# Linear attention and a squared-ReLU layer: the first product's last two blocks placed among the small steps of A11 B11

## The chip, the core and the metric

The kernel runs on one core of one Trainium2 chip. The metric is the device time of one execution in microseconds, as the median of three runs. The profile is of one further execution.

## What is computed

Linear attention over 8 batches, 8 heads, 576 positions and heads of 64, its normed result as the 4608 x 512 input of a layer with a squared ReLU:

```python
kv = np.einsum('bhsd,bhse->bhde', k, v)
out = np.einsum('bhsd,bhde->bhse', q, kv)
rms = np.sqrt(np.mean(out * out, axis=-1, keepdims=True) + 1e-06)
attn = (out / rms * g_norm).astype(np.float32)
x = np.ascontiguousarray(attn.transpose(0, 2, 1, 3)).reshape(B * S, H * D)
h = x @ w_in                  # 4608 x 512 by 512 x 2048
r = np.maximum(h, 0.0)
g = s * (r * r) + b
return (g @ w_out).astype(np.float32)   # 4608 x 2048 by 2048 x 512
```

Everything is fp32. In the profile a matrix product of `x` with `w_in` is the first product, and that of the squared ReLU with `w_out` the second; `s` and `b` are folded in where the second product is drained.

## The kernel before

**Units.** The 4608 rows are worked through in nine units of 512 rows, u = 0 to 8. Each unit has its first product (`mm1`) and then its second (`mm2`); between the pieces of the second product of unit u stands the attention for the rows of unit u + 1. Unit 8 has no next unit, and so no attention.

**Both products are cut into seven.** Instead of the eight products of a 2 x 2 block matrix product the kernel makes seven, from sums and differences of blocks. The seven are numbered 1 to 7 and run in the order 1, 2, 6, 7, 5, 3, 4. They share three PSUM accumulators: x takes 1, 6, 5 and 3 one upon the other, z takes 2, and y takes 7 and 4. Between two of them VectorE or ScalarE drains the state of x that belongs to an output block. The names of the steps say which accumulator they use: `x1`, `z2`, `x6`, `y7`, `x5`, `x3`, `y4`.

**The first product** of a unit goes over four column strips s = 0 to 3. In a strip each of the seven is a group of eight TensorE instructions with 256 columns. Its results are four blocks, `a11`, `a12`, `a21`, `a22`, and each becomes its own squared ReLU on VectorE: `a11` comes out of z2, `a22` out of x5 (an addition in L594 of PSUM accumulator y and a kept copy `r4`, and a square in L595, whose helper is L523), `a21` out of x3 and `a12` out of y4. The kept copies `r1`, `r2`, `r4` are made by ScalarE (L568). From the blocks the second product needs sums as well: `s1` = a21 + a22, and x3's last line turns a21 into a11 - a21. In strips 0 to 2, x3 and y4 of a strip are put between the steps of the next strip. Strip 3 has no next strip: there its x3 and y4 are put into the second product.

**The second product** of units 2 to 8 is cut into seven once more for four of its seven (1, 2, 7 and 4), in the function `second_level`. These small products have groups of eight instructions with 128 columns, and what they sum up is made on VectorE by `sums` into a ring of five tiles called `sub`. The text below calls the first of the four (block 1 of the upper level, from a11) A11 B11, its program name is `p1`, and the second (block 2, from a12) A12 B21, program name `p2`. Step m of `p1` is `p1[m]`. `sums` makes four operands, for the steps 5, 6, 7 and 3. A drain is one VectorE operation in L660; its results are `r` (kept for a later drain) or `o` (a part of the output).

**The order of the work** is written out by hand: the program's order is the order on each engine, and each engine works through its own queue. A wait comes in only where an operand or a buffer requires it. In units 2 to 8 the end of the first product of strip 3 and the start of the second product were:

```python
def sums_ahead():            # after y7 of strip 3, ahead of x5
    p1["sums"]()
    turn[0]()
    turn[1]()
```

Then came x5 of strip 3; then A11 B11's steps 1, 2, 6, 7 and 5; then x3 and y4 of strip 3, each with all of its VectorE work at once; then A11 B11's step 3, A12 B21's sums for 5 and 6, step 4, attention's product for the next unit (`product_q[0]`, with a square on ScalarE and a reduction on VectorE), A12 B21's step 1, the sum for 7, step 2, the sum for 3, step 6, and so on. `turn` is the turning of a part of q on VectorE (L391).

**Weights of the second product** come from device memory into a ring of seven tiles, in the order in which they are used. `pump(2)` puts two loads into SyncE's queue; each waits until TensorE is done with the tile that it overwrites. A group of attention matmuls in the timeline is L421.

Of the kernel before, what the change touches and what calls it, by code (L numbers as in the profile page):

```python
# [1 line left out]

# [8 lines left out]
AF = mybir.ActivationFunctionType  # L11
# [4 lines left out]
def kernel(  # L16
# [39 lines left out]
    nc = tc.nc  # L56
# [171 lines left out]
    def add(o, a, b):  # L228
        nc.vector.tensor_tensor(out=o, in0=a, in1=b, op=ALU.add)  # L229

    def sub(o, a, b):
        nc.vector.tensor_tensor(out=o, in0=a, in1=b, op=ALU.subtract)  # L232
# [274 lines left out]
    ga, g_pair = {}, {}  # L507
    bank = {}

    def bank_of(key, tag, bufs=2):  # L510
        bank[key] = ps_f.tile([P, 2, TB], FP32, name=f"{tag}_ps", tag=tag, bufs=bufs)
        return bank[key]
# [9 lines left out]
    def relu_sq(t):  # L522
        nc.vector.scalar_tensor_tensor(t, t, 0.0, t, ALU.max, ALU.mult)  # L523

    def g_tile(name, s):
        if s % 2 == 0:
            g_pair[name, s // 2] = gp.tile([P, 2, 2, TB], FP32, name=name, tag=name)
        ga[name, s] = g_pair[name, s // 2][:, s % 2]
        return ga[name, s]

    def g_s1(s):
        add(ga["s1", s], ga["a21", s], ga["a22", s])
# [29 lines left out]
    def mm1(u, s):  # L562

        st = {}

        def keep(name, src, tag):
            st[name] = rp.tile([P, 2, TB], FP32, name=name, tag=tag)
            nc.scalar.copy(st[name], src)  # L568

        def x1():  # L570
            st["x"] = bank_of("x", "x")
            mm1_product(1, u, s, st["x"], True)
            keep("r1", st["x"], "ra")

        def z2():
            ps = bank_of("z", "z", 1)
            mm1_product(2, u, s, ps, True)
            t = g_tile("a11", s)
            add(t, ps, st["r1"])
            relu_sq(t)  # L580

        def x6():
            mm1_product(6, u, s, st["x"], False)
            keep("r2", st["x"], "rb")

        def y7():
            st["y"] = bank_of("y", "y")
            mm1_product(7, u, s, st["y"], True)

        def x5():  # L590
            mm1_product(5, u, s, st["x"], False)
            keep("r4", st["x"], "ra")
            t = g_tile("a22", s)
            add(t, st["y"], st["r4"])  # L594
            relu_sq(t)  # L595

        def x3():
            mm1_product(3, u, s, st["x"], False)
            t = g_tile("a21", s)
            nc.scalar.activation(t, st["x"], AF.Relu)  # L600
            nc.vector.tensor_mul(t, t, t)  # L601
            g_tile("s1", s)
            g_s1(s)
            sub(ga["a21", s], ga["a11", s], ga["a21", s])

        def y4():
            mm1_product(4, u, s, st["y"], False)
            t = g_tile("a12", s)
            add(t, st["y"], st["r2"])
            relu_sq(t)  # L610

        return dict(x1=x1, z2=z2, x6=x6, y7=y7, x5=x5, x3=x3, y4=y4)

# [5 lines left out]
    def twice(u, i):  # L621
        return u > 1 and i in TWICE
# [5 lines left out]
    def pump(k):  # L628

        for u, i, n in queue_w2[:k]:  # L630
            t = late["ring"].tile([P, 4 * HN], FP32, name="w2_sb", tag="w2")
            if twice(u, i):
                t = t.rearrange("p (m f n) -> p m f n", m=2, n=P)
                k2 = min(2, 7 - 2 * n)
                nc.sync.dma_start(out=t[:, :k2], in_=w3_dram[i][:, 2 * n : 2 * n + k2])
            else:
                t = t.rearrange("p (f n) -> p f n", n=HN)
                nc.sync.dma_start(out=t, in_=w2_dram[i][:, 4 * n : 4 * n + 4])
            ring[u, i, n] = t
        del queue_w2[:k]  # L640
# [2 lines left out]
    out_18 = out.rearrange("(b t j) n -> b j t n", t=32, j=JC)  # L643
    G_OF = {1: "a11", 2: "a12", 3: "a12", 4: "a22", 5: "s1", 6: "a11", 7: "a21"}

    def mm2(u, att=None):

        st = {}

# [241 lines left out]
        def right(name, j, q=slice(0, HN)):  # L891
            return rows(name, j)[:, HN:][:, q]

        p1 = second_level(1, lambda j, q: b2[:, q], lambda j, q: right("o1", j, q), "x")
        p2 = second_level(2, lambda j, q: right("o1", j, q), lambda j, q: rows("o1", j)[:, q])
# [36 lines left out]
            turn[0]()  # L932
            turn[1]()

        def first():
            for m in (1, 2, 6, 7, 5):
                p1[m]()
            pump(2)

        def second():  # L940
            p1[3]()
            p2["sums"]((5, 6))
            p1[4]()
            pump(2)
            product_q[0]()
            p2[1]()
            p2["sums"]((7,))
            p2[2]()
            p2["sums"]((3,))
            p2[6]()  # L950
            s2((0, 1))
            p2[7]()
            p2[5]()
            s2((2, 3))
            pump(2)
            norm[0]()
            p7["sums"]()
            x6_of(0)
            p2[3]()
            p2[4]()  # L960
            for j in range(2):
                left = rows("o1", j)[:, :HN]
                add(left, left, b_12)
            pump(2)
            attend(1)
            turn_x[0]()
            turn[2]()
            x6_of(1)
            pump(2)
            p7[1]()  # L970
            s4((0,))
            p7[2]()
            p7[6]()
            s4((1,))
            p7[7]()
            s4((2,))
            p7[5]()
            s4((3,))
            pump(2)
            attend(2)  # L980
            turn_x[1]()
            turn[3]()
            x5_of(0)
            p7[3]()
            with_7(0)
            p7[4]()
            pump(2)
            attend(3)
            turn_x[2]()
            x5_of(1)  # L990
            with_7(1)
            turn_x[3]()
            pump(2)
            p4["sums"]()
            x3(0)
            for m in (1, 2, 6, 7, 5):
                p4[m]()
            pump(2)
            x_sums_next[0]()
            x3(1)  # L1000
            pump(2)
            y4_of(0, 3)
            y4_of(1, 4)
            pump(2)

        return [sums_ahead, first, second]


    NU = FC // 2
# [158 lines left out]
    for u in range(U):  # L1168
        if u > 0:
            loads(u)  # L1170
        steps = [mm1(u, s) for s in range(NS)] if u > 0 else []
        slots = []
        for s, a in enumerate(steps):
            slots.append(a["x1"])
            if s:
                slots.append(steps[s - 1]["x3"])
            slots.append(a["z2"])
            if s:
                slots.append(steps[s - 1]["y4"])
            slots += [a["x6"], a["y7"], a["x5"]]  # L1180
        if u == 0:
            first_unit()
        side = side_of(u)
        second = mm2(u, side if u > 1 else None)
        if u > 1:
            ahead, *second = second
        for n, slot in enumerate(slots):
            slot()
            if u > 1 and n == len(slots) - 2:
                ahead()  # L1190
            if u == 1 and n in (1, 3, 5):
                for sums in sums_w_in((n + 1) // 2):
                    sums()
            if u in kv_due and n == 12:
                kv_product(kv_due[u])
            elif u + 1 in kv_due and n == 14:
                for i in range(2):
                    load_kv(kv_due[u + 1], i, late["kv"], tag="kv")
        if u > 1:
            side = {}  # L1200
        for n, slot in enumerate(second):
            slot()
            if u == 0:
                if n == 1:
                    for i in range(2):
                        load_kv(1, i, convp, tag="raw", bufs=3)
                    store_w2(1)
                    loads(0)
                    store_w2(5)
                elif n == 2:  # L1210
                    t2 = convp.tile([P, 4 * R * D], FP32, name="w_t2", tag="raw", bufs=3)
                    W2_AT[6] = t2[:, : FC // 2 * HN].rearrange("p (f n) -> p f n", n=HN)
                    for i in range(14, 16):
                        more(i)
                    sub_w_out(6, 3, 5)
                    store_w2(3, 2, 6)
            if n == 0 and u > 0:
                for step in ("x3", "y4"):
                    steps[-1][step]()
            for step in side.get(n, []):  # L1220
                step()
        if u == 0:
            tc_late()
            for i in range(2):
                load_kv(kv_due[1], i, late["kv"], tag="kv")
            pump(7)
# [30 lines left out]
```

## Time and profile before

| what | value |
|---|---|
| median of three runs | 966.7 us (965.61 to 966.81) |
| profiled run, its span on the core | 966.18 us, 964.3 us |
| granted TensorE clock, mean | 0.999 |
| TensorE matmuls, weight loads | 943.5 us (98%), 840.8 us (87%) |
| VectorE | 612.1 us (63%), 1100 instructions |
| ScalarE | 194.3 us (20%) |
| DMA | 151.09 MB, mean 157 GB/s |

A weight load (PEld in the profile) stands ahead of each matmul (PE) and overlaps the one before. In a line of the timeline the first number is the start in us, the second the time until the end of the last of the merged instructions, and x8 says that eight of them are merged; the bracket at the end, where there is one, is the idle time of that engine just before, and who ended it. In a line of the waits the three numbers are the total in us, how often, and the longest. Nearly all matmuls and additions are issued in helper functions (L90, L229, L232, L523, L660), so an instruction is told by its tiles: `y_ps<-xs,wb` is step 7 or 4 of the first product, `x_ps<-xT,ws` step 3 of it, `x_ps<-w_sb,a` and `x_ps<-w_sb,sub` are steps of the second product.

### The profile page before, as it was taken

Reading aid. Unit: us, or ns where it says so; the run is one execution under the profiler, and the core shown is the slowest. Engines: PE = TensorE matmul, PEld = TensorE weight load, DVE = VectorE, ACT = ScalarE, POOL = GpSimd, SP = SyncE. Lnnn points to the kernel's source line nnn. Section 1 sums busy time; section 2 is a strip of 40 time slices with the busy share of each in tenths; the row PEclk is TensorE's granted clock in tenths of the full one; section 3 lists DMA queues with packets and bytes.
Section 4 is the critical chain, followed back from the end, with each engine's and each line's share of the span. In section 5 each row is a group of like instructions: output and inputs, shape, how many; then the busy total and the mean of one; then the engine's idle time right before and its main releaser. Section 6 shows DMA issues by size and latency. Waiting matters only on the chain. (4 is left out here: it accounts for less than half of the span.)

```text
span 964.3 us, 17222 instructions
## 1 busy us (share of the span) xinstructions
PE 943.5 (98%) x7102; PEld 840.8 (87%) x7102; DVE 612.1 (63%) x1100; ACT 194.3 (20%) x366; POOL 6.7 (1%) x18
## 2 busy tenths in 40 slices
PE   7999999999999999999999999999999999999997
PEld 7888888888888898889888988899888988898897
DVE  2789767575548854786368735874488557864573
ACT  2773132101221111111210212021211111111100
POOL 2000000000000000000000000000000000000000
PEclk9999999999999999999999999999999999999999
DMA  9688829577754566155355555456135531551163
GB/s 243 203 280 251 269 77 276 114 227 247 204 107 132 180 196 131 51 195 180 91 121 177 187 138 115 127 191 182 27 95 182 181 68 52 190 188 53 33 207 99
DMA packets 131709, 151.09 MB, mean 157 GB/s; under 512 B 76592, under 2 KB 89136, under 8 KB 131504
## 3 DMA queue, kind: packets, MB, share of 16 engines
q1 hardware_dynamic: 128528, 148.22, 53.7%
q10 hardware_dynamic: 2784, 1.77, 0.8%
q8 instruction: 56, 0.92, 0.4%
q14 instruction: 21, 0.17, 0.1%
q0 software_dynamic: 320, 0.00, 0.0%
HBM read 125.83 MB, written 24.12 MB: 155 GB/s over the span
## 5 line engine op out<-in xcount | busy, mean ns | idle before, releaser
L90 PE MATMUL x_ps<-w_sb,a 128*128 128x256 f32 (+1 forms) x600 | 130.9, 371 | 0.0
L568 ACT COPY r<-x_ps 128x512 f32<-128x512 f32 x96 | 56.2, 585 | 332.4 <-PE x_ps L90 325.7
L90 PEld LDWEIGHTS x_ps<-w_sb,a 128*128 128x128 f32 x600 | 108.6, 190 | 15.2 <-issue 1.6
L90 PE MATMUL x_ps<-xs,ws 128*128 128x256 f32 x512 | 121.0, 379 | 0.0
L90 PE MATMUL y_ps<-xs,wb 128*128 128x256 f32 x512 | 120.9, 379 | 0.0
L90 PEld LDWEIGHTS x_ps<-xs,ws 128*128 128x128 f32 x512 | 97.3, 190 | 13.2
L90 PEld LDWEIGHTS y_ps<-xs,wb 128*128 128x128 f32 x512 | 97.3, 190 | 13.2
L229 DVE TENSOR_TENSOR a<-y_ps,r 128x512 f32<-128x512 f32 x64 | 44.0, 688 | 97.2 <-ACT r L568 96.4
L90 PE MATMUL y_ps<-w_sb,sub 128*128 128x128 f32 x728 | 90.0, 276 | 3.1 <-DVE r L660 3.1
L90 PEld LDWEIGHTS y_ps<-w_sb,sub 128*128 128x128 f32 x728 | 86.8, 192 | 5.5 <-DVE r L660 4.4
L90 PE MATMUL x_ps<-xT,wa 128*128 128x256 f32 x384 | 89.6, 380 | 0.1
L90 PEld LDWEIGHTS x_ps<-xT,wa 128*128 128x128 f32 x384 | 72.3, 190 | 10.2 <-ACT xT L470 0.5
L90 PE MATMUL y_ps<-w_sb,a 128*128 128x128 f32 (+1 forms) x472 | 70.3, 294 | 0.0
L523 DVE SCALAR_TENSOR_TENSOR a<-a 128x512 f32<-128x512 f32 x96 | 66.4, 692 | 3.3
L601 DVE TENSOR_TENSOR a<-a 128x512 f32<-128x512 f32 x32 | 22.1, 692 | 72.3 <-ACT a L600 72.3
L90 PEld LDWEIGHTS y_ps<-w_sb,a 128*128 128x128 f32 x472 | 63.8, 191 | 4.2 <-DVE o L660 1.2
L90 PE MATMUL x_ps<-xT,ws 128*128 128x256 f32 x256 | 61.1, 382 | 0.0
L90 PE MATMUL z_ps<-xT,wa 128*128 128x256 f32 x256 | 60.5, 379 | 0.0
L90 PE MATMUL x_ps<-w_sb,s 128*128 128x256 f32 x256 | 59.1, 384 | 0.0
L90 PEld LDWEIGHTS x_ps<-w_sb,s 128*128 128x128 f32 x256 | 47.4, 190 | 8.4 <-issue 2.6
L90 PEld LDWEIGHTS z_ps<-xT,wa 128*128 128x128 f32 x256 | 48.6, 190 | 6.6
L90 PEld LDWEIGHTS x_ps<-xT,ws 128*128 128x128 f32 x256 | 47.6, 190 | 6.3
(126 smaller groups left out, 1060.3 us busy)
## 6 DMA issues: line engine op xcount, KB each, us to landing
w_sb<-w SPq DMA_DIRECT2D x140, 512.0 KB, 4.3
kv_sb<-in_k_dram SPq DMA_DIRECT2D x30, 288.0 KB, 5.0
kv_sb<-in_v_dram SPq DMA_DIRECT2D x30, 288.0 KB, 6.2
w_raw<-in_moe_w_in_dram SPq DMA_DIRECT2D x8, 1024.0 KB, 7.1
w_raw<-in_moe_w_out_dram SPq DMA_DIRECT2D x8, 1024.0 KB, 5.7
w_sb<-w SPq DMA_DIRECT2D x28, 256.0 KB, 2.8
out_dram<-o SPq DMA_DIRECT2D x104, 64.0 KB, 1.8
q_sb<-in_q_dram SPq DMA_DIRECT2D x144, 32.0 KB, 2.2
```

The costliest lines, as they stand in the source:

```text
L90: nc.tensor.matmul(o, lhsT=lhsT, rhs=rhs, start=start, stop=stop, skip_group_check=True)
L229: nc.vector.tensor_tensor(out=o, in0=a, in1=b, op=ALU.add)
L523: nc.vector.scalar_tensor_tensor(t, t, 0.0, t, ALU.max, ALU.mult)
L568: nc.scalar.copy(st[name], src)
L601: nc.vector.tensor_mul(t, t, t)
```

## The change

In units 2 to 8 the order from x5 of strip 3 on is written anew. y4 of strip 3 goes between the steps 2 and 6 of A11 B11, and x3 stays behind step 5, now behind the `pump`. The VectorE work of the two is taken apart: of y4 the addition and the square (`y4_square`) are two pieces, and of x3 the ReLU, the square (`x3_square`), the sum s1 (`x3_s1`) and the difference (`x3_s3`) are four. The four sums of A12 B21 are made in one go behind x3. Strips 0 to 2, and the units 0 and 1, run the same pieces one after the other as before.

```diff
         def x3():
             mm1_product(3, u, s, st["x"], False)
-            t = g_tile("a21", s)
-            nc.scalar.activation(t, st["x"], AF.Relu)
-            nc.vector.tensor_mul(t, t, t)
+            nc.scalar.activation(g_tile("a21", s), st["x"], AF.Relu)
+
+        def x3_square():
+            nc.vector.tensor_mul(ga["a21", s], ga["a21", s], ga["a21", s])
+
+        def x3_s1():
             g_tile("s1", s)
             g_s1(s)
+
+        def x3_s3():
             sub(ga["a21", s], ga["a11", s], ga["a21", s])

         def y4():
             mm1_product(4, u, s, st["y"], False)
-            t = g_tile("a12", s)
-            add(t, st["y"], st["r2"])
-            relu_sq(t)
+            add(g_tile("a12", s), st["y"], st["r2"])
+
+        def y4_square():
+            relu_sq(ga["a12", s])
...
-        def first():
-            for m in (1, 2, 6, 7, 5):
-                p1[m]()
+        def all_of_it():
+            p1[1]()
+            p1[2]()
+            step["y4"]()
+            p1[6]()
+            step["y4_square"]()
+            p1[7]()
+            p1[5]()
             pump(2)
-
-        def second():
+            step["x3"]()
+            p2["sums"]()
             p1[3]()
-            p2["sums"]((5, 6))
+            step["x3_square"]()
             p1[4]()
+            step["x3_s1"]()
             pump(2)
             product_q[0]()
             p2[1]()
-            p2["sums"]((7,))
+            step["x3_s3"]()
             p2[2]()
-            p2["sums"]((3,))
             p2[6]()
             s2((0, 1))
             p2[7]()
```

The rest of the difference passes strip 3's steps into `mm2`, and calls the two parts `sums_ahead` and `all_of_it` from the loop over units.

More of the change, by code (lines that the diff above doesn't have):

```diff
@@ L1 @@
 from contextlib import ExitStack
+from functools import partial
 import concourse.bass as bass
@@ L607, in y4 @@
             mm1_product(4, u, s, st["y"], False)
-            t = g_tile("a12", s)
-            add(t, st["y"], st["r2"])
-            relu_sq(t)
-        return dict(x1=x1, z2=z2, x6=x6, y7=y7, x5=x5, x3=x3, y4=y4)
+            add(g_tile("a12", s), st["y"], st["r2"])
+        def y4_square():
+            relu_sq(ga["a12", s])
+        return dict(
+            x1=x1, z2=z2, x6=x6, y7=y7, x5=x5, x3=x3, x3_square=x3_square, x3_s1=x3_s1,
+            x3_s3=x3_s3, y4=y4, y4_square=y4_square,
+        )
     ring = {}
@@ L644, with mm2 @@
     G_OF = {1: "a11", 2: "a12", 3: "a12", 4: "a22", 5: "s1", 6: "a11", 7: "a21"}
-    def mm2(u, att=None):
+    def mm2(u, step=None, att=None):
         st = {}
@@ L1004, in second @@
             pump(2)
-        return [sums_ahead, first, second]
+        return sums_ahead, all_of_it
     NU = FC // 2
@@ L1171, with x3, y4 @@
         steps = [mm1(u, s) for s in range(NS)] if u > 0 else []
+        def x3(a):
+            for name in ("x3", "x3_square", "x3_s1", "x3_s3"):
+                a[name]()
+        def y4(a):
+            for name in ("y4", "y4_square"):
+                a[name]()
         slots = []
@@ L1175 @@
             if s:
-                slots.append(steps[s - 1]["x3"])
+                slots.append(partial(x3, steps[s - 1]))
             slots.append(a["z2"])
             if s:
-                slots.append(steps[s - 1]["y4"])
+                slots.append(partial(y4, steps[s - 1]))
             slots += [a["x6"], a["y7"], a["x5"]]
@@ L1183 @@
         side = side_of(u)
-        second = mm2(u, side if u > 1 else None)
-        if u > 1:
-            ahead, *second = second
+        second = mm2(u, steps[-1], side) if u > 1 else mm2(u)
         for n, slot in enumerate(slots):
@@ L1189 @@
             if u > 1 and n == len(slots) - 2:
-                ahead()
+                second[0]()
             if u == 1 and n in (1, 3, 5):
@@ L1199 @@
         if u > 1:
-            side = {}
+            second[1]()
+            continue
         for n, slot in enumerate(second):
@@ L1217 @@
             if n == 0 and u > 0:
-                for step in ("x3", "y4"):
-                    steps[-1][step]()
+                x3(steps[-1])
+                y4(steps[-1])
             for step in side.get(n, []):
```

## The prediction

> **What bounds the kernel now.** I read the page's busy times first, then the list of waits of TensorE's weight loads, then the timeline at the seven places that the change touches.
>
> ```profile
> PE 943.5 (98%) x7102; PEld 840.8 (87%) x7102; DVE 612.1 (63%) x1100; ACT 194.3 (20%) x366; POOL 6.7 (1%) x18
> ```
>
> TensorE is the bound: 943.5 of 964.3 us. VectorE has 612.1, so it costs only where TensorE stands and waits for one of its results. The waits say where:
>
> ```profile
> PEld x_ps L90 <- DVE r L660: 6.0, 7, 0.9
> ...
> PEld y_ps L90 <- DVE r L660: 4.4, 7, 1.0
> ...
> PEld y_ps L90 <- DVE o L660: 1.2, 6, 0.2
> ```
>
> Seven units (u = 2 to 8) use the two-level second product, and each stops twice on a "r" that VectorE drains out of PSUM. The third row is no loss to win: 0.20 us follows every group of attention matmuls (L421), whatever comes after it. The first stop, in unit 2:
>
> ```profile
> 294.93 0.58 ACT L568 COPY r<-x_ps 128x512 f32<-128x512 f32 x1 [2.92 <-PE x_ps L90]
> 295.46 0.97 PEld L90 LDWEIGHTS z_ps<-w_sb,a 128*128 128x128 f32 x8
> 295.55 0.69 DVE L229 TENSOR_TENSOR a<-y_ps,r 128x512 f32<-128x512 f32 x1
> ...
> 296.27 0.69 DVE L523 SCALAR_TENSOR_TENSOR a<-a 128x512 f32<-128x512 f32 x1
> ...
> 296.88 0.35 DVE L660 SCALAR_TENSOR_TENSOR r<-x_ps,s_col,b_row 128x128 f32<-128x128 f32 x1
> 297.28 0.97 PEld L90 LDWEIGHTS x_ps<-w_sb,sub 128*128 128x128 f32 x8 [0.85 <-DVE r L660]
> ```
>
> The bank of small step 1 is ready early, but its drain stands in VectorE's queue behind the block a22 (L229, L523), which had to wait for the end of x5 and ScalarE's copy. Unheld groups of 128 columns start 0.89 us apart (298.17, 299.06), so small step 6 was due at 295.46 + 0.89 = 296.35 and started at 297.28: stop A, 0.93 us. The second stop:
>
> ```profile
> 306.55 0.60 ACT L430 ACTIVATE xn<-x_ps 128x512 f32<-128x512 f32 x1 [3.96 <-PE x_ps L421]
> ...
> 307.86 0.68 DVE L432 TENSOR_REDUCE ss<-xn 128x8 f32<-128x512 f32 x1
> 308.45 0.34 DVE L660 SCALAR_TENSOR_TENSOR r<-y_ps,s_col,o 128x128 f32<-128x128 f32 x1
> ...
> 308.85 2.75 PEld L90 LDWEIGHTS y_ps<-w_sb,sub 128*128 128x128 f32 x24 [0.58 <-DVE r L660]
> ```
>
> Due at 307.29 + 0.89 = 308.18, started at 308.85: stop B, 0.67. VectorE is in a jam here: eight large operations start between 302.62 and 307.86, and the drain of step 1 of A12 B21 stands behind them. Unit 8 has no attention for a next unit to fill TensorE, and its B is larger:
>
> ```profile
> 917.02 2.09 PEld L90 LDWEIGHTS y_ps<-w_sb,a 128*128 128x128 f32 x16
> 919.03 0.97 PEld L90 LDWEIGHTS z_ps<-w_sb,a 128*128 128x128 f32 x8
> 920.98 2.75 PEld L90 LDWEIGHTS y_ps<-w_sb,sub 128*128 128x128 f32 x24 [0.97 <-DVE r L660]
> ```
>
> B is 920.98 - 919.92 = 1.06, and 16 loads took 2.09 in place of 1.86: 0.23 that small step 1 of A12 B21 waited for its bank, which y4's addition (917.41 to 918.09) holds. A is the same 0.93 in all seven (0.85 idle in each), B is 0.67 in six. In all 7 x 0.93 + 6 x 0.67 + 1.06 + 0.23 = 11.8 us.
>
> [...] step 6 stood still with y4's operands long in place, and the drain of step 1 waited behind a22. [...] the trace has 692 for the additions of s1 and 684 where an operand comes from PSUM. [...] the count of instructions stays, so cutting the chain between them adds nothing.
>
> **The change, part by part.** No arithmetic is added or removed. On TensorE one group of eight moves: y4's product, from behind x3 to between small steps 2 and 6. On VectorE a12's addition goes behind step 2's drain and its square behind step 6's; all four sums of A12 B21 go ahead of the drain of step 3; a21's square, s1 and difference are spread behind steps 3, 4 and 1. ScalarE's and SyncE's queues keep their order, GpSimd has nothing in these units, and neither y4 nor x3 issues a DMA.
>
> TensorE, unit 2, by start of group. A group of 256 columns behind one of 128 is followed after 1.63 (299.95 to 301.58), the next of 128 after 0.99 (303.31 to 304.30). Step 1 at 294.46, 2 at 295.46, y4 at 296.35, 6 at 297.98, 7 at 298.97, 5 at 299.86, x3 at 300.75, 3 at 302.38, 4 at 303.37, attention at 304.47 (1.10 later, as before), then steps 1, 2, 6 of A12 B21 at 305.48, 306.37, 307.26. Before, the last one was at 308.85: 1.59 gained if nothing holds.
>
> What could hold it. (1) y4 writes the bank that a22's addition reads, a wait that it did not meet before. The addition ends at 296.24, TensorE follows VectorE by 0.05 (297.23 to 297.28): 296.29 against 296.35. Queued behind y4 are steps 6, 7, 5. The margin is 0.06, so zero to 0.1. (2) Step 6 needs step 1's drain, still done at 297.23, against 297.98: free by 0.70. This is what removes A. (3) a12's addition waits for the end of y4, about 0.41 after the next group starts (301.58 to 301.99 for x3), so at 298.39, and stands ahead of step 6's drain. That is due at 298.97 + 0.31 = 299.28; VectorE is free again at 299.00. (4) Step 5 needs it at 299.86, it ends 299.63. The square fits between it and step 5's drain (301.06). (5) From there VectorE starts each operation as the trace shows: 0.26 after a small one, 0.60 to 0.61 after a large independent one, 0.72 where the next needs the result. Drains 301.06 and 301.45, sums 301.71, 302.43, 303.04, 303.64, drain 304.25, square 304.51, drain 305.12, s1 305.38, VectorE free at 305.99. (6) Now attention's square: 1.15 after the group starts (305.40 to 306.55), so 305.62; it ends 306.22, the reduction starts 306.25 and the drain of step 1 at 306.84, done 307.19. Step 6 may start at 307.24, due 307.26. B is gone with 0.02 to spare, so zero to 0.1 left. From here on both kernels have the same order with TensorE leading.
>
> The sums find their buffers: five in the ring, and the last three take those of steps 5, 6, 7 of A11 B11, ended by 301.1. The weight loads: the second tile for block x6 behind A12 B21 takes the place that step 3 frees (303.7), and is used at 311.7: 8.0 us in unit 2, and by the same count 7.1 in unit 8 (916.4 to 923.5). The longest landing of this kind in the trace is 5.8. Hidden.
>
> Unit 8, the same walk without attention: steps 5, x3, 3, 4 at 912.58, 913.47, 915.10, 916.09; steps 1, 2, 6 at 916.98, 917.87, 918.76. Drain of 5 at 913.79, sums 914.44 to 916.96, drain, square 917.22, drain, s1 918.09, drain of step 1 at 918.70, done 919.05, so step 6 at 919.10: 0.34 is left of B; the bank wait of 0.23 goes. Gain 920.98 - 919.10 = 1.88.
>
> Sum: 6 x 1.59 + 1.88 = 11.4; for the two margins I take off 0.1 in all, 11.3. The span of 964.3 becomes 953.0. The profiled run took 966.2, and the three timed ones 965.6 to 966.8 with median 966.7; taken off that, 955.4. A difference of 0.2% (2 us) is about what a measurement of this kernel can tell.
>
> **Rivals.** First, B stays: if VectorE goes throughout at its slowest shown spacing (0.39 behind a small operation, 0.73 behind a large one), the walk from 301.06 ends with step 6 at 308.13, a gain of 0.72 in place of 1.59, and in unit 8 at 920.13, a gain of 0.85: 6 x 0.72 + 0.85 = 5.2, so 961.5. Half way is 958.5. For it: the margin is 0.02. Against: the short spacings are in the trace for the same pairs of sizes. Second, y4's new wait takes the place of A: if VectorE has been kept by the two q transposes ahead of a22 (294.12 for 1.30, so until 295.42, against ScalarE's end of 295.51), the wait could grow by tenths; at most A comes back whole, 6.5 less, 960. Against: same instructions ahead as before. Third, slower: TensorE without pauses loses granted clock. [...] here one core runs, at 0.999, and between 210 and 285 us TensorE was busy for 75.00 of 75 us at a granted clock of 1.00. The point is a clock of 0.988, where 1.2% is lost; at 0.98 it ends at 955.4 x 0.999/0.98 = 974. Fourth, no change: the stops move to another place behind; nothing there is short in either order.
>
> **How the numbers follow.** Forecast 0.77 (954.2 to 956.4), B or A partly back 0.15 (to 961.5), no change 0.03, slower 0.05. Faster is 0.92. The range, 953.9 to 959.8, starts at all 11.8 won with the spread of the runs and reaches over more than half of the second case.
>
> **What would show it.** In the trace after, the weight loads' wait for "r" should fall from 10.4 us to under 1, unit 8 holding most of it; y4's loads should stand between z_ps and x_ps steps; unit starts should be 1.6 us closer together. A wait of y_ps for L229 over 0.1 per unit would prove (1) wrong; a "y_ps <- DVE r" of 0.5 in each unit, (5) or (6); equal waits gone but the same span, the whole reading.

## The result and the profile after

The changed kernel took 954.62 us (954.17 to 956.60) against 966.15 for the kernel before (965.34 to 966.81), medians of four executions with the profiled one counted in: a ratio of 0.9885, 95% interval 0.9868 to 0.9902, or 11.5 us less. The forecast was 955.4.

The helpers stand one line lower than before, the drain eleven lines (L660 is L671 now). The page's first line of busy times, and the one line on a drained "r" that the list of the weight loads' waits still has (total in us, times, longest):

```profile
PE 939.9 (98%) x7102; PEld 839.9 (88%) x7102; DVE 611.3 (64%) x1100; ACT 194.5 (20%) x366; POOL 6.7 (1%) x18
```

```profile
PEld y_ps L91 <- DVE r L671: 0.2, 1, 0.2
```

The same 1100 instructions of VectorE with about the same busy time (611.3 us, 612.1 before); 10.4 us of waits have become 0.2. (The 1.2 us on a drained "o" is no longer put down to VectorE, but the pause of 0.20 behind the attention matmuls is still there, as forecast: in unit 2 the load at 307.33 has it.) The two places in unit 2, from the timeline (start, time to the end of the last, instruction, idle before and releaser):

```profile
297.30 0.97 PEld L91 LDWEIGHTS z_ps<-w_sb,a 128*128 128x128 f32 x8
297.39 0.69 DVE L230 TENSOR_TENSOR a<-y_ps,r 128x512 f32<-128x512 f32 x1
...
298.20 1.60 PEld L91 LDWEIGHTS y_ps<-xs,wb 128*128 128x128 f32 x8
...
298.73 0.34 DVE L671 SCALAR_TENSOR_TENSOR r<-x_ps,s_col,b_row 128x128 f32<-128x128 f32 x1
...
299.82 1.08 PEld L91 LDWEIGHTS x_ps<-w_sb,sub 128*128 128x128 f32 x8
...
308.10 0.69 DVE L433 TENSOR_REDUCE ss<-xn 128x8 f32<-128x512 f32 x1 [0.19 <-ACT xn L431]
...
308.70 0.34 DVE L671 SCALAR_TENSOR_TENSOR r<-y_ps,s_col,o 128x128 f32<-128x128 f32 x1
...
309.11 2.76 PEld L91 LDWEIGHTS y_ps<-w_sb,sub 128*128 128x128 f32 x24
```

Unit 2's step 1 starts at 296.31 here and at 294.46 before, so the forecast's walk, its list of start times, has to be moved by 1.85. y4 starts at 298.20 (walk: 298.20), with no wait on a22's addition. The drain of step 1 is as late as ever behind that addition, but while it runs TensorE is at y4; step 6 follows at 299.82 (walk: 299.83) and no weight load waited. At the second place attention's square on ScalarE holds the reduction for 0.19, the drain follows at 308.70 (308.69), and step 6 of A12 B21 starts at 309.11 (309.11), just when it is due. Unit 8 keeps the one wait, 11.91 us behind its step 1 where the walk had 11.92:

```profile
910.25 0.97 PEld L91 LDWEIGHTS z_ps<-w_sb,a 128*128 128x128 f32 x8
911.46 2.75 PEld L91 LDWEIGHTS y_ps<-w_sb,sub 128*128 128x128 f32 x24 [0.23 <-DVE r L671]
```

The kv groups of two units that follow each other were 102.94 us apart (269.86, 372.80) and are 101.36 apart (271.71, 373.07): 1.58 per unit. The profiled span, 954.8, is only 9.5 below that of before. The rest is the 1.85 by which unit 2 began later in this one execution, for reasons that lie ahead of any changed instruction. Two weight loads from the start of the kernel before, and the same two after the change:

```profile
22.98 0.42 PEld L458 LDWEIGHTS xT_ps<-ident,xn 128*128 128x128 f32 x4 [2.32 <-ACT w_raw L209]
23.80 0.47 PEld L400 LDWEIGHTS z_ps<-ident,q_sb 128*128 128x128 f32 x4
```

```profile
24.45 0.42 PEld L459 LDWEIGHTS xT_ps<-ident,xn 128*128 128x128 f32 x4 [3.96 <-ACT w_raw L210]
25.49 0.87 PEld L401 LDWEIGHTS z_ps<-ident,q_sb 128*128 128x128 f32 x4
```

The wait for ScalarE's weight preparation was 1.64 longer, and behind it the granted clock was 0.66 from 25 to 30 us (1.00 before the change), so that the work up to the next long group took 4.95 us in place of 3.76. A start 0.17 earlier, and a later wait for VectorE that was 0.8 shorter, take part of this back. From 40 to 950 us the clock was 1.00 in every stretch. The spans of the three other executions were 952.4, 952.7 and 952.8, where the forecast said 953.0.

### The profile page after: what moved, and what is told of

It is laid out like the page before. It is cut to its first block, busy times and chain, and to the rows that moved or that the text cites. A ratio compares the mean times of both kernels' runs of the same rounds, so it can differ in the third digit from the quotient of the medians.

```text
span 954.8 us, 17222 instructions
## 1 busy us (share of the span) xinstructions
PE 939.9 (98%) x7102; PEld 839.9 (88%) x7102; DVE 611.3 (64%) x1100; ACT 194.5 (20%) x366; POOL 6.7 (1%) x18
## 4 chain that ended last, share of the span: by engine, by line
PE 95%; DMA 2%; DVE 1%; ACT 1%; issue 0%; SPq 0%; ACTq 0%; DVEq 0%
PE x_ps L91 49%; PE y_ps L91 32%; PE z_ps L91 9%; PE x_ps L422 3%; PE kv_ps L360 2%; DMA w_raw<-in_moe_w_in_dram 1%; DMA kv_sb<-in_k_dram 1%; PE qT_ps L401 0%; DVE xn L441 0%; DVE xT L465 0%; ACT xT L471 0%; ACT w_raw L210 0%; ACT w_raw L205 0%; SPq L103 0%; DVE wb L225 0%
```

## The experiments

Times are compared as ratios to the kernel before, run on the same chip as each experiment; on these chips that took 963.8 to 964.3 us. A thousandth is 0.96 us.

**TensorE's order alone (e1_order_only).**

```diff
             step["y4"]()
+            step["y4_square"]()
             p1[6]()
-            step["y4_square"]()
...
             step["x3"]()
-            p2["sums"]()
+            step["x3_square"]()
+            step["x3_s1"]()
+            step["x3_s3"]()
             p1[3]()
+            p2["sums"]((5, 6))
...
             p2[1]()
+            p2["sums"]((7,))
             p2[2]()
+            p2["sums"]((3,))
```

> TensorE's new order alone: y4 between steps 2 and 6, but y4's addition and square together, x3's four pieces together, and the sums of A12 B21 in three parts as in the kernel before. Theory (the stop is a place in VectorE's queue): A goes, but 0.26 comes back ahead of step 5 (the square delays step 6's drain), and B grows to 1.06 in units 2 to 7, because VectorE now stands idle from step 5's drain until x3 is through and then has everything at once. Step 6 of A12 B21 at 308.58 on unit 2's clock in place of 308.85: 0.27 gained in each of seven units, 1.9 us in all, so about 964.3. Rival (the move on TensorE is the whole gain): as the changed kernel, about 954.6.

Ratio 0.9985 (0.9978 to 0.9991), 1.4 us faster (0.9 to 2.1), against 1.9 of the theory and 11.5 of the rival. The timeline of weight loads in unit 2 of this kernel:

```profile
297.70 0.97 PEld L91 LDWEIGHTS y_ps<-w_sb,sub 128*128 128x128 f32 x8
298.85 0.97 PEld L91 LDWEIGHTS x_ps<-w_sb,sub 128*128 128x128 f32 x8 [0.18 <-DVE r L671]
...
305.35 0.97 PEld L91 LDWEIGHTS z_ps<-w_sb,a 128*128 128x128 f32 x8
307.30 2.75 PEld L91 LDWEIGHTS y_ps<-w_sb,sub 128*128 128x128 f32 x24 [0.98 <-DVE r L671]
```

Step 5 is 0.26 late (298.85 against 297.70 + 0.89) and step 6 of A12 B21 1.06 (307.30 against 305.35 + 0.89), both as worked out. Most of the stop has moved from A to B: the move on TensorE alone is worth little.

**VectorE's order alone (e2_pieces_only).**

```diff
-            step["y4"]()
             p1[6]()
-            step["y4_square"]()
...
             step["x3"]()
+            step["y4"]()
+            step["y4_square"]()
             p2["sums"]()
```

> VectorE's new order alone: x3 and y4 back behind step 5 on TensorE, the pieces and the four sums as in the changed kernel, the sums behind y4's square. Theory: A stays at 0.93; y4's addition can only start at 303.72 on unit 2's clock and all else queues behind it, so that the drain of step 1 ends at 310.37 and step 6 starts at 310.42, 1.57 later than before; the same 1.57 in unit 8. Seven times that is 11.0 us slower than before, about 977. Rival (pieces alone free the queue): B goes and A stays, about 961.

Ratio 1.0184 (1.0165 to 1.0203): 17.7 us slower. The rival falls. The theory has the sign, but 11.0 is short by more than a third. Weight loads at step 6 of A12 B21, in unit 2 and in unit 3:

```profile
308.48 2.75 PEld L91 LDWEIGHTS y_ps<-w_sb,sub 128*128 128x128 f32 x24 [2.15 <-DVE r L671]
...
412.99 4.38 PEld L91 LDWEIGHTS y_ps<-w_sb,sub 128*128 128x128 f32 x24 [2.15 <-DVE r L671]
```

In unit 2 all is as forecast: due at 306.24, 2.24 late, then 24 loads in 2.75 us. Unit 3 has the same pause, but then the same 24 loads take 4.38. The table of windows, the same 14 us around this place in units 2 and 3 (busy times and counts of PE, PEld, DVE, ACT and POOL, then the granted clock, DMA share, GB/s), has the granted clock at 1.00 and at 0.88:

```profile
304.00:318.00 14.00, 12.04 (x126) 10.84 (x119) 13.27 (x29) 1.16 (x3) 0.00 (x0) 1.00 0.51 164
408.50:422.50 14.00, 12.04 (x91) 11.19 (x84) 11.64 (x24) 0.90 (x2) 0.00 (x0) 0.88 0.48 147
```

TensorE's granted clock fell in four of the seven units (3, 4, 6 and 8; 0.88 over 14 us in each), and the 24 loads took longer there: 3 x 1.63 and once 1.33 (4.08 in place of 2.75), 6.2 us. With 11.3 us more of waits (15.7 in place of 4.4) this makes 17.5. In the other three units (2, 5 and 7) a pause of 2.15 was followed by 24 loads in 2.75, at a clock of 1.00; at the same place the pause of 1.59 us in unit 8 of e1 was followed by 24 loads in 2.75 as well. That the longer pause brings the clock down is not shown.

What this run shows holds for this order of VectorE, in which the sums stand behind y4's late square. No run tried the other one: TensorE's order as before, with only the sums for 5 and 6 brought forward. VectorE had room for them, from 301.00 to this line in unit 2 of the kernel before:

```profile
302.62 0.69 DVE L601 TENSOR_TENSOR a<-a 128x512 f32<-128x512 f32 x1 [1.62 <-ACT a L600]
```

An estimate from that trace: the two sums take about 1.3 us, so behind them the reduction would wait only for attention's square, which ends at 307.15. With the spacings of the prediction (0.03, 0.60, 0.35 and 0.05) step 6 could then start at 308.18, just when it was due. B, 6 x 0.67 + 1.06 = 5.1 us before, might so go without moving y4.

**y4's square at once (e3_square_at_once, e9_square_again).**

```diff
             step["y4"]()
+            step["y4_square"]()
             p1[6]()
-            step["y4_square"]()
```

> The changed kernel with y4's square straight behind its addition, ahead of step 6's drain. Theory: the square (0.72 behind the addition, 0.61 itself) brings step 6's drain to an end at 300.07 on unit 2's clock, where step 5 is due at 299.86: a wait of 0.26 in each of seven units, 1.8 us, so about 956.4. Rival (the margin ahead of step 5 is wider than 0.2, or the pause is taken in later): no wait, 954.6.

> The kernel with y4's square straight behind its addition once more, beside the changed kernel. Theory: 0.26 in each of seven units, 1.8 us slower than the changed kernel. Rival: the same time.

Ratio 0.9895 (0.9878 to 0.9912), then 0.9908 (0.9893 to 0.9922). The changed kernel beside the second:

> The changed kernel itself, on the same chip as the next two, so that small differences can be read. Expected 0.9885 of the kernel before.

It had 0.9885 (0.9871 to 0.9900) once more, 952.48 us against 954.82. The intervals overlap, so the times alone leave it open; the weight loads do not, with this line in unit 2 and its like in all seven (1.2 us in the list of waits):

```profile
297.09 0.97 PEld L91 LDWEIGHTS x_ps<-w_sb,sub 128*128 128x128 f32 x8 [0.18 <-DVE r L671]
```

The load before it started at 295.94, so it is 0.26 late, as expected.

**The sums at their old places (e4_sums_as_before).**

```diff
             step["x3"]()
-            p2["sums"]()
             p1[3]()
+            p2["sums"]((5, 6))
             step["x3_square"]()
...
             p2[1]()
+            p2["sums"]((7,))
             step["x3_s3"]()
             p2[2]()
+            p2["sums"]((3,))
```

> The changed kernel with the sums of A12 B21 in three parts at their old places: 5 and 6 behind step 3, 7 behind step 1, 3 behind step 2. Theory: VectorE is idle from step 5's drain (301.7) to step 3's (303.7), and the two sums come into the way later: step 1's drain is done at 307.69, step 6 starts at 307.74 where it was due at 307.26, so 0.48 in six units and 0.77 more in unit 8: 3.7 us, about 958.3. Rival (where the sums stand is of no account once y4 has moved): 954.6.

Ratio 0.9950 (0.9935 to 0.9965): 6.3 us slower than the changed kernel, where 3.7 was expected. The expected stop is there, and a second that the expectation had not looked for:

```profile
305.25 1.86 PEld L91 LDWEIGHTS y_ps<-w_sb,sub 128*128 128x128 f32 x16 [0.39 <-DVE r L671]
307.57 0.97 PEld L91 LDWEIGHTS y_ps<-w_sb,sub 128*128 128x128 f32 x8 [0.46 <-DVE r L671]
```

Step 6 is 0.48 late (305.25 against 303.88 + 0.89). Then step 5 of A12 B21 waits, too, as two sums, the difference and a drain stand ahead of step 6's drain (it starts at 307.16): 0.54 late against 305.25 + 2 x 0.89. In all the list of waits has 6.6 us on a drained "r", where the changed kernel has 0.2. So, once y4 has moved, bringing the four sums forward into VectorE's idle time, 301.7 to 303.7 on the walk's clock, is over half of the gain.

**y4 one group earlier (e5_y4_ahead_of_2).**

```diff
             p1[1]()
-            p1[2]()
             step["y4"]()
+            p1[2]()
```

> The changed kernel with y4 one group earlier, between steps 1 and 2 of A11 B11. Theory (y4 waits for a22's addition, the new wait of the change): y4 is due at 295.46 on unit 2's clock and can't start before the addition has ended, at 296.29, so 0.83 is lost in each of seven units, 5.8 us, about 960.4, with a wait of y_ps for L230 in the list. Rival (the bank isn't what holds it, any filler group ahead of step 6 is as good): 954.6.

Ratio 0.9950 (0.9933 to 0.9967), 6.3 us slower than the changed kernel. In unit 2:

```profile
293.85 1.08 PEld L91 LDWEIGHTS x_ps<-w_sb,a 128*128 128x128 f32 x8
295.68 1.59 PEld L91 LDWEIGHTS y_ps<-xs,wb 128*128 128x128 f32 x8 [0.76 <-DVE a L230]
```

0.84 late against 293.85 + 0.99, and the releaser is a22's addition. The new wait is real; the place behind step 2 is the first where it costs nothing.

**x3's difference early (e6_s3_early).**

```diff
             step["x3_s1"]()
+            step["x3_s3"]()
...
             p2[1]()
-            step["x3_s3"]()
             p2[2]()
```

> The changed kernel with x3's difference straight behind s1, ahead of attention's reduction and of the drain of step 1 of A12 B21. Theory (VectorE's slack there is 0.26 ahead of the reduction and about 0 behind): 0.61 more in front brings the reduction from 306.25 to 306.60 on unit 2's clock and leaves a wait of about 0.33 at step 6 in six units, and 0.61 more in unit 8: 2.6 us, about 957.2. Rival (there is room): 954.6.

Ratio 0.9916 (0.9902 to 0.9931), 3.0 us slower than the changed kernel. In unit 2:

```profile
303.77 0.97 PEld L91 LDWEIGHTS z_ps<-w_sb,a 128*128 128x128 f32 x8
305.09 2.75 PEld L91 LDWEIGHTS y_ps<-w_sb,sub 128*128 128x128 f32 x24 [0.34 <-DVE r L671]
```

0.43 late, 0.1 more than the walk's 0.33, because the difference starts 0.72 behind s1 (303.49 behind 302.77) where the walk counted 0.61: one more large operation in front and the margin is overdrawn.

**The last wait of unit 8 (e7_last_s1_later, e10_last_s1_again).**

```diff
-            step["x3_s1"]()
+            if u < U - 1:
+                step["x3_s1"]()
             pump(2)
             product_q[0]()
             p2[1]()
+            if u == U - 1:
+                step["x3_s1"]()
             step["x3_s3"]()
```

> The changed kernel, with s1 behind the drain of step 1 of A12 B21 in unit 8 alone, where there is no attention to wait for. Theory: the last wait left at step 6 (0.23 idle, about 0.3 against its due time) goes, and nothing else moves: 954.3, which the times cannot tell from 954.6 but the list of waits can (no wait of y_ps for a drained r at all). Rival (something else holds step 6 in unit 8): the wait stays.

> The kernel with s1 behind the drain of step 1 in unit 8 alone, beside the changed kernel: 0.3 us faster by the list of waits, which is below what the times can tell. Rival (the order in unit 8 costs elsewhere): slower by more than 1 us.

Ratios 0.9884 (0.9868 to 0.9901) and 0.9891 (0.9875 to 0.9908), against 0.9885 of the changed kernel. In the list of waits no line with a drained "r" is left, in either run. The third of a microsecond shows in the trace and cannot be seen in the times: the second median, 953.57, is even 1.1 us above the changed kernel's 952.48 beside it, which is past the rival's mark, though the intervals overlap. The traces settle it for unit 8: from its step 1 to the start of its last drain there are 49.91 us in the changed kernel (e8) and 49.60 in both of these runs, so the order costs nothing elsewhere in the unit. In the times, no version is shown to beat the changed kernel.

## Why the prediction was right

**The bound.** Right: the end of the two stops accounts for the gain, 1.58 per unit and 1.89 in unit 8 (13.80 from its step 1 to the late step 6 before, 11.91 after), 6 x 1.58 + 1.89 = 11.4 in all.

**A, by y4 as a filler.** Right, with its condition: y4 needs a22's addition (e5), and there was a margin of 0.06 that held in all seven units. The 0.1 us that the sum took off for the two margins was not needed. That the times give 11.5 where the working has 11.4 is partly luck, as the interval of the ratio reaches from 9.5 to 12.8 us; the firm agreement is that of the start times in the trace.

**B, by VectorE's order.** Right, and the larger lesson. The second rival had A coming back through the new wait, which did not happen. (Its most is also worked out wrongly: 955.4 and 6.5 make 961.9, not 960. Nothing hung on it.) What the runs show is that with VectorE's old order most of the stop that y4 fills comes back at the next drain (e1). The new place for the sums is over half of the gain (e4), and the square's (e3) and the difference's (e6) are worth 0.26 and 0.43 per unit.

**The spacing of VectorE's operations.** The first rival's slow spacing did not come up. The short one (in unit 8 from 906.54 on 0.26 to 0.27 us behind a small operation, 0.60 to 0.61 behind a large one, 0.72 from the first sum to the second, which takes its result) held to 0.01 us from the drain of step 5 to the drain of step 1: in unit 8 without a break, in units with attention up to the reduction, which waits for ScalarE (0.19 in unit 2).

**The clock.** The third rival had a clock that falls when TensorE has no more pauses. The changed kernel had 1.00 throughout from 40 to 950 us. Where the traces show a fall of the clock that cost time, in e2 (0.88 over 14 us) and at the start of the profiled execution of the changed kernel (0.66 from 25 to 30 us), it stood behind pauses, of 2.15 to 2.77 us and of 3.96: in these runs the rival's sign was wrong. The pauses that the change left at the two stops are 0.23 at most.

**The weight tiles** never held a step, as taken: the list of the weight loads' waits after the change has no wait for a DMA.

## What to carry to other kernels

In these traces TensorE stood still at a wait, and the work behind it stood too: 0.85 us at step 6 of A11 B11 in the kernel before, 0.76 at y4 in e5. Before such a wait, look for work whose inputs have long been there, and put that ahead (the sums on VectorE), and put work that nobody awaits soon behind the next drain (the square, the difference). When a filler moves on the bounding engine, set the order on the draining engine anew for it; the move alone gave 1.4 us less, and the new order without the move 17.7 us more, where both gave 11.5 less. That every order on the draining engine needs the move is not shown: the sums alone were not tried. Write out the start of every operation between two waits from the durations of the trace: in the changed kernel that was good to 0.01 us, and it names the margin that breaks first. In e4 the walk was ended one group too early, and so missed a second wait about as long as the first.

## What the runs showed of the hardware

In e2 four of seven pauses of 2.15 to 2.77 us were followed by weight loads at 4.08 to 4.38 us for 24 in place of 2.75, with a granted clock of 0.88 over 14 us; three pauses of 2.15 were not (2.75, at a clock of 1.00). At the start of the kernel the clock was 0.66 from 25 to 30 us behind a pause of 3.96 (the changed kernel), and 1.00 in the same stretch behind one of 2.32 (the kernel before). The length of a single pause doesn't tell the six of 2.15 us in e2 apart, and what does stays open. Four pauses of TensorE in e2 so came with 1.33 to 1.63 us more in the loads behind them, on top of their own length.
